# Part of the output stored early, two buffers for the P rows, phases on ScalarE and a new written order, in a kernel that mixes two long convolutions

## The chip, the cores and the metric

The kernel runs on one core of one Trainium2 chip. The core has five engines that run side by side: TensorE (PE, with its weight loads shown as PEld), VectorE (DVE), ScalarE (ACT), GpSimd (POOL) and SyncE (SP, which here only issues DMAs), and 16 DMA engines that they share. The metric is the device time of one execution in microseconds (us). The kernel before took 279.8 us, the median of three runs (279.80, 280.59 and 277.46).

## The reference

For an input x of 2048 rows and 448 channels, the reference computes two long causal convolutions along the rows and mixes them with a gate:

```
g = sigmoid((x * gate_w).sum(-1))                       # one gate per row
K[d, l] = Re sum_n C[d,n] * exp(dt[d]*A[d,n]*l) * dt[d]*B[d,n]     # 256 modes, 2048 taps
a = irfft(rfft(x, 4096) * rfft(K, 4096))[:2048] + x * Dskip
kv = (sum over t of k shifted by t rows * shift_k[:, 3 - t ...]) * v   # 4 taps
b = x * (irfft(rfft(kv, 4096) * rfft(ssm_k, 4096))[:2048] + kv * ssm_D)
out = g * a + (1 - g) * b
```

A is complex, so K needs an exponential and a sine and cosine for every channel, mode and level. Below, "A" names the convolution whose taps K the kernel must generate, and "B" the one whose taps ssm_k come as an input.

## The kernel before

The 448 channels lie as 4 groups of 112 on 4 x 32 partitions. The 112 columns of a group are worked in 4 chunks of 28 (`NQG`, `NC`), so there are eight convolutions, B and A of each chunk. A convolution is done by TensorE as a factored Fourier transform: `spread` (first stage, PSUM tile `ps_c`), `transform` (second stage, `ps_2`), a product with the transformed taps on VectorE (`products`, which also needs a copy of the tile with its real and imaginary halves exchanged by DMA, `swapped`), then the inverse, `stage_a` (`ps_a`) and `stage_b` (`ps_b`). ScalarE carries nearly every PSUM tile to SBUF. The tiles between the stages, 128 x 32 x 112 in bf16 (names `zs`, `zsS`, `zsK`, `U`), share one pool of `NBQ` = 7 buffers. The temporary tiles of the front part use it too.

The taps K of A come in 8 blocks of 14 columns (`KGen.block`). A chunk of two blocks has its tables of exponentials and phases (`Tables.levels`, `Tables.reals`): for each power level a phase is made on VectorE as an integer turn (`unit`, tile `ks_ph`, or `ks_ph4` for the first chunk), its low 16 bits go through a Sin on ScalarE, and VectorE multiplies with the Exp. From them VectorE builds two factor tables, the Q rows (`kg_TQ`, once in a chunk) and the P rows (`kg_TP`, once in a block, 32 rows of 2 x 112), and TensorE multiplies the two (`pk`). P rows 8 to 15 are a sum of two products: VectorE writes both, and a DMA issued by GpSimd adds one onto the other. Rows 16 to 31 (`back`) are made from rows 0 to 15. There is one P tile, so a block's rows cannot be written while the matmuls of the block before it still read them. `gather` (`ps_g`) rounds the taps into place, and `spread` with `WcK` starts their transform.

The inverse's matrix G (`Consts.stage_b`) is made in the front from eight phase instructions (`sb_ph`), four Sin and sixteen masks. The gate's two factors are `gb` and `og`; `mix` scales and adds the A and B results of the first three chunks in place, in tile `vt` (also called `ug`). The last convolution, A of chunk 3, runs in halves; its epilogue adds to the last 28 columns, 16 rows of each partition at a time, and `store` then writes those rows with all 112 columns, on SyncE and ScalarE in turns.

The sequence of all of this is written out by hand. Every engine call is first collected in a list by `Order`, and `ORDER` names the list's indices in the sequence in which they are issued; each engine then runs its own instructions in just that sequence, waiting where data are not there. All instructions therefore have line 148, and the profile is read by the names of tiles.

Of the kernel before, what the change touches and what calls it, by code (L numbers as in the profile page):

```python
# [9 lines left out]
ACT = mybir.ActivationFunctionType  # L10
# [28 lines left out]
NBQ = 7  # L39
# [3 lines left out]
    "0-1 540 2 945 947 23 886 559 533 553-554 896-897 560 31 13 544 538 542-543 967 36 946 539 546 549 60 12 551 22 "  # L43
    "561 563 565 569 955 562 8 970 566 61 953-954 25 62-68 572-580 831 934 931 928 529 3 930 938 7 564 53 34-35 557 "
    "601-605 568 606-609 32 582-589 33 30 531 962 541 545 548 581 4 9 17 29 936 958 591 914 905 44 889 907 550 887 "
    "941 590 874 851 878 527-528 11 555 850 864 968 956 926 833 556 619-623 929 830 592-599 860 863 924 855 28 927 "
    "829 600 843 859 836 835 834 610-614 14 24 839 948 898-899 949 877 530 942 842 837 950 832 933 838 27 615-617 "
    "932 923 957 879 16 624-627 618 854 847 873 960 861 963 875 628 865 868 26 20 70 41 848 631 535 844-845 18 880 "
    "567 532 840 849 906 964 69 630 470-497 19 937 629 299-326 925 888 883 558 959 876 852-853 916 185-212 915 866 "
    "856-857 965 858 890 869-870 547 891 882 862 867 908 1500 498-525 42 900 570 871 917 885 918 872 327-354 841 971 "  # L50
    "213-240 43 961 966 881 355 55 552 241 10 15 5 21 6 951 526 356-411 58 939 534 536 38 242-297 884 128-155 57 56 "
    "943 412 909 846 39 952 537 298 2873 2887 2883 40 571 2884 46 413-440 1478 2885 441-469 2896 37 54 632 935 "
    "156-184 2888 71-98 2895 2877 99-127 910 892 921 913 2878 911 2876 940 912 1480 47 684-692 893 920 903 650-666 "
    "633-648 667-679 919 680-682 649 683 765-771 895 772-781 1479 2882 48 45 748-764 711-719 731-737 720-727 738-746 "
    "728 782-789 894 969 747 1151-1164 790 1483 1165-1166 901 904 1125-1140 1486 922 1481 1167 902 49 51 1142-1150 "
    "1141 791-799 693-701 1491 1202-1209 702-710 944 1108-1124 1482 2874 1502 1210 1168-1181 1501 1182-1183 "
    "1091-1103 1484 1503 1104-1106 52 50 1184-1191 1107 809-816 1489 1192-1200 817 800-807 1201 59 972-1001 1504 "
    "1271-1278 808 1002-1016 1279 1490 1505 2875 1298-1305 1487 1017-1031 1306 1506 1032-1046 1493 1307-1315 1507 "
    "1047-1061 818-826 1494 1508 1062-1084 2880 1316-1323 1495 729 1085-1086 1324 1492 2563-2569 1325-1333 2570-2578 "
    "1496 2579 1485 1883-1890 1499 1891 1849-1862 1488 1498 1476 1497 2879 1510 1863-1864 2881 1334-1342 730 2889 "  # L60
    "1509 1511 1280-1287 1289-1296 1512-1543 1865 1297 2897 1544-1639 1473 828 1640-1703 2900 1704-1735 1288 2899 "
    "2901 827 2118-2119 2904 1736 2905-2906 2120 1245-1261 2909 2121 2908 2910 2919 2122 2918 2123 1228-1244 "
    "1262-1269 2892 1270 2920 2124 2886 1211-1218 1474 2893 2126 1475 2125 2890 1219-1227 2911 2128 1477 2922 "
    "2537-2544 1755-1794 2545 2902 2520-2535 1795 1408-1439 2907 2536 2486-2502 2898 2894 2503-2519 2903 1440-1455 "
    "1828 1456-1471 2923 1737-1753 2924 1343-1358 2912 2921 1359-1390 2914 2913 1391-1406 1472 2127 1754 1866-1872 "
    "2915 2891 1829 2946 2928 2927 2129 2937 1814-1821 2969 2943 1873-1879 2938 2934-2935 2933 2666-2673 2929 2674 "
    "2916-2917 2940 1407 2930 1880-1882 2925 2130-2161 1831 2162-2193 1830 2194-2225 1832-1845 2675-2682 1846-1848 "
    "2683 2947 2944 2226-2353 2948 2971 1909-1916 1822 2949 2932 1823-1826 2354 2926 2970 1827 1952-1960 2945 2941 "
    "1805-1812 1943-1951 2693-2701 1917-1925 2931 2952 1892-1907 1926-1941 2942 2972 1813 1942 2936 2955 1908 "
    "2546-2552 2973 2553-2561 4620-4626 2958 2974 1796-1803 2959 4627-4628 2684-2691 2597-2604 2975 2939 2562 2605 "  # L70
    "1804 2692 2580-2595 2962 2950 2373-2413 1961-1968 1970-1977 2596 1969 1978 2711-2718 2355-2371 2702-2709 2719 "
    "4145 4153 2720-2727 2963 2951 2961 2053-2068 2710 2069-2116 2964 2976 2965 2372 2977 2728 2979 4149 2729-2737 "
    "2432-2439 4152 2440 2968 2953 1988-2019 2966 4148 4151 4147 2960 2954 2020-2035 4186 4150 3298 2117 2423-2431 "
    "2956 2967 2036-2051 2978 3318-3324 2980 4146 2957 4176 3352-3359 4154 3360 2981-3044 4177 3587 4185 4187 3297 "
    "3045-3076 3300 3299 2441-2444 3077-3108 4167 2445 4178 2870 3325-3334 4168 1979-1987 4169 2414-2422 3109-3172 "
    "4160 4159 4161 3173-3205 2466-2473 2052 4180 3589 3588 2474 3361-3368 4165 4164 4166 3412-3420 3590 3395-3402 "
# [968 lines left out]
```

## Time and profile before

| | |
|---|---|
| median of three runs | 279.8 us |
| the profiled execution, and its span | 277.69 us, 275.8 us |
| busy: DVE, ACT, PE, PEld, POOL | 241.7, 226.7, 210.7, 193.3, 15.9 us |
| packets of all DMAs | 55110, 24.74 MB; 49680 of them under 512 bytes |
| stores of the output | 16 DMAs of 112 KB, 8 by SyncE and 8 by ScalarE |
| P rows' adding DMA (`kg_TP<-kg_P`) | 8 DMAs of 448 KB, 5.7 us from issue to landing |
| loads of ScalarE's function tables | 11, 1283 ns each |

The page of a profile gives busy time by engine, then a line of 40 digits for each engine, in which a digit is the busy share of a fortieth of the span in tenths. Groups of instructions are listed as out<-in with the number of instructions, their busy time and the mean duration of one. A list of waits says which instruction stood, what it waited for, the total in us, how many times and the longest. A timeline line is start, duration, engine, operation.

### The profile page before, as it was taken

What the parts mean: (1) busy time and instruction counts of PE and PEld (TensorE: products, weight loads), DVE (VectorE), ACT (ScalarE), POOL (GpSimd) and SP (SyncE); (2) the same over time, 40 slices, a digit from 0 to 9 for tenths busy, and PEclk for the clock granted to TensorE, in tenths of its full rate; (3) what the DMA queues carried; (4) which work ended last, traced back from release to release, by engine and by line L of the source; (5) the groups of instructions that cost most, each with busy time, mean ns of one, the idle gap of its engine ahead of it and who ended that gap; (6) DMA issues with size and microseconds to landing.
All of it is one profiled execution on the core that took longest, in us unless ns stands there. A gap on an engine that the chain in (4) does not pass through costs nothing.

```text
span 275.8 us, 12739 instructions
## 1 busy us (share of the span) xinstructions
PE 210.7 (76%) x5770; PEld 193.3 (70%) x5770; DVE 241.7 (88%) x488; ACT 226.7 (82%) x383; POOL 15.9 (6%) x51
## 2 busy tenths in 40 slices
PE   0610958879988799798997789867887999699830
PEld 0500858877887798687995779766886899688820
DVE  7599899999989799979996899899999997967950
ACT  2795696999899999998998799999999989546400
POOL 8000000000400000100010001001001001000000
PEclk9999999999999899998998999999999999979975
DMA  7999799607804500390093019003042263600077
GB/s 149 224 204 172 131 235 175 99 1 153 118 5 91 116 5 4 83 186 5 5 209 47 5 50 199 10 2 70 6 90 64 54 138 60 147 5 2 2 141 127
DMA packets 55110, 24.74 MB, mean 90 GB/s; under 512 B 49680, under 2 KB 52368, under 8 KB 55056
## 3 DMA queue, kind: packets, MB, share of 16 engines
q1 hardware_dynamic: 48640, 19.34, 37.7%
q0 software_dynamic: 1152, 3.67, 7.2%
q10 hardware_dynamic: 5264, 0.92, 2.1%
q8 instruction: 45, 0.74, 1.2%
q14 instruction: 9, 0.07, 0.1%
HBM read 7.95 MB, written 2.87 MB: 39 GB/s over the span
## 4 chain that ended last, share of the span: by engine, by line
ACT 38%; PE 29%; DVE 15%; DMA 9%; issue 5%; SPq 0%; DVEq 0%; POOL 0%; POOLq 0%; ACTq 0%
ACT zs L148 15%; ACT ET L148 7%; ACT U L148 6%; DMA kg_TP<-kg_P 6%; PE pk L148 5%; PE ps_a L148 5%; PE ps L148 5%; PE ps_c L148 5%; PE ps_b L148 5%; ACT zsK L148 5%; DVE vt L148 2%; DVE scratch L148 2%; PE ps_g L148 2%; PE ps_gate L148 2%; DMA skraw<-in_B_ssm_k_dram 2%
## 5 line engine op out<-in xcount | busy, mean ns | idle before, releaser
L148 ACT CAST zs<-ps 128x896 bf16<-128x896 f32 x48 | 44.0, 944 | 1.0 <-PE ps L148 0.6
L148 ACT CAST zs<-ps_c 128x1024 bf16<-128x1024 f32 (+1 forms) x48 | 42.7, 937 | 1.3 <-PE ps_c L148 1.2
L148 PEld LDWEIGHTS <-front 128*32 128x32 bf16 (+1 forms) x496 | 19.1, 159 | 27.3 <-issue 22.3
L148 PEld LDWEIGHTS <-s_W 128*128 128x128 bf16 x544 | 28.9, 100 | 12.7 <-issue 9.6
L148 PE MATMUL pk<-kg_TP,kg_TQ 128*32 128x32 bf16 x1792 | 33.2, 242 | 5.1 <-issue 2.9
L148 PEld LDWEIGHTS <-kg_TQ 128*32 128x32 bf16 x1792 | 31.2, 160 | 7.0 <-issue 4.8
L148 PE MATMUL ps_a<-sa_R,zs 128*128 128x128 bf16 x224 | 32.7, 235 | 0.3
L148 ACT CAST U<-ps_a 128x1024 bf16<-128x1024 f32 (+1 forms) x30 | 27.2, 936 | 6.9 <-PE ps_a L148 6.7
L148 PE MATMUL ps_b<-U,sb_G 128*128 128x28 bf16 x1024 | 29.5, 175 | 4.1 <-issue 1.4
L148 PE MATMUL ps_a<-sa_R,zsS 128*128 128x128 bf16 x224 | 32.1, 232 | 0.5 <-DVE zsS L148 0.5
L148 PE MATMUL ps<-zs,s_W 128*128 128x112 bf16 x384 | 27.7, 220 | 5.5 <-ACT zs L148 4.2
L148 PEld LDWEIGHTS <-sb_G 128*128 128x128 bf16 x1024 | 27.8, 96 | 5.8 <-issue 3.2
L148 DVE TENSOR_TENSOR kg_TP<-kg_TP,ET 128x1792 bf16<-128x1792 bf16 x24 | 26.1, 1090 | 5.8 <-DMA kg_TP<-kg_P 5.0
L148 PEld LDWEIGHTS <-zsS 128*128 128x128 bf16 x224 | 29.6, 152 | 1.3 <-DVE zsS L148 0.7
L148 PEld LDWEIGHTS <-zs 128*128 128x128 bf16 x224 | 29.4, 151 | 0.8
L148 PE MATMUL ps_v<-front 128*32 128x336 bf16 (+3 forms) x448 | 16.0, 310 | 16.0 <-DVE front L148 13.1
L148 ACT ACTIVATE ET<-ks_ph 128x448 bf16<-128x448 int16 x40 | 23.2, 602 | 4.1 <-DVE kg_P L148 2.6
L148 DVE TENSOR_TENSOR kg_TQ<-kg_TQ,ET 128x896 bf16<-128x896 bf16 (+1 forms) x36 | 24.8, 730 | 0.0
L148 DVE TENSOR_TENSOR kg_P<-kg_TP,ET 128x1792 bf16<-128x1792 bf16 (+1 forms) x24 | 22.4, 934 | 0.1
L148 PE MATMUL ps_c<-Wc,uu 128*64 128x128 bf16 x224 | 18.4, 290 | 1.6 <-ACT U L148 0.6
L148 PE MATMUL ps_c<-Wc,vt 128*64 128x128 bf16 x224 | 17.1, 285 | 1.4 <-ACT zs L148 1.2
L148 PEld LDWEIGHTS <-uu 128*64 128x64 bf16 x224 | 16.5, 210 | 2.4 <-issue 1.5
(102 smaller groups left out, 427.4 us busy)
## 6 DMA issues: line engine op xcount, KB each, us to landing
zsS<-zs SPq DMA_DIRECT2D x16, 448.0 KB, 5.7
kg_TP<-kg_P POOLq DMA_DIRECT2D x8, 448.0 KB, 5.7
vt<-in_B_v_dram SPq DMA_DIRECT2D x4, 448.0 KB, 6.8
skraw<-in_B_ssm_k_dram SPq DMA_DIRECT2D x16, 112.0 KB, 4.8
uu<-in_A_u_dram SPq DMA_DIRECT2D x4, 448.0 KB, 8.5
ks_xf<-xfd SPq DMA_DIRECT2D x3, 336.0 KB, 3.3
out_dram<-vt ACTq DMA_DIRECT2D x8, 112.0 KB, 3.8
out_dram<-vt SPq DMA_DIRECT2D x8, 112.0 KB, 3.6
```

Source lines behind the costliest of these rows:

```text
L148: ins = f(*args, **kw)
```

## The change

1. `store` writes only the last 28 columns of the rows that are just done. The 84 columns of the first three chunks are written by four new DMAs on SyncE at the end of `mix`.
2. One P tile of 48 rows takes the place of one of 32: rows 0 to 15 exist twice, by the block's parity, rows 16 to 31 (`late`) once. The pool of big tiles goes from 7 buffers to 6.
3. In the last block, rows 8 to 15 are made as the lower rows are, with two products and two sums on VectorE, and no DMA.
4. The phases of the first chunk's tables (20 instructions) and of G (8) are computed by ScalarE as a scaled and shifted copy, with the shifts in four constants that GpSimd sets; 12 negations in the tables and the four additions of ssm_D to the loaded ssm_k go to VectorE, from ScalarE and GpSimd.
5. `ORDER` is a new sequence of the 6767 calls (6758 before). The reading of it here is by index: calls up to the last block's P rows moved by 4, later ones by 5, those after `mix` by 9.

```diff
-NBQ = 7
+NBQ = 6
...
+        self.turns = {x: self.carve(1).bitcast(f32) for x in (0.0, QUARTER, 8192.0, 8192.0 + QUARTER)}
+        for x, t in self.turns.items():
+            nc.gpsimd.memset(t, x)
...
-                self.phases(ph[:, :, r, :], jv, k_col, o)
+                nc.scalar.activation(ph[:, :, r, :], jv, ACT.Identity, scale=k_col[:, 0:1], bias=o)
...
+    def summed(self, dst, src, r, m):
+        n = src.shape[1]
+        part = self.pool.tile([P, 8 * 2 * M], bf16, name="kg_P4", tag="kg_P4", bufs=2)[:, 0:n * 2 * m]
+        for c, out in enumerate((part.rearrange("p (n v m) -> p n v m", n=n, v=2), dst)):
+            self.nc.vector.tensor_tensor(out=out, in0=src[:, :, c].unsqueeze(2).to_broadcast([P, n, 2, m]),
+                                         in1=bass.AP(r.tensor, r.offset + c * m, [list(r.ap[0]), [0, n], [-m, 2], [1, m]]), op=ALU.mult)
+        self.nc.gpsimd.dma_start(dst.rearrange("p n v m -> p (n v m)"), part, accum_op=ALU.add)
...
-        TP = self.pool.tile([P, 32, 2, M], bf16, name="kg_TP")
+        if j == 0:
+            self.TA = self.pool.tile([P, 48, 2, M], bf16, name="kg_TP")
+        TP, late = self.TA[:, 16 * (j % 2):16 * (j % 2) + 16], self.TA[:, 32:48]
+        far = 16 * (2 - j % 2)
...
-            V.tensor_tensor(out=TP[:, 16 + i0:16 + i1], in0=src,
+            V.tensor_tensor(out=late[:, i0:i1], in0=src,
...
+        if j == NBLK - 1:
+            add(8, mult(TP[:, 0:4], 64))
+            add(12, mult(TP[:, 4:8], 64))
+        else:
+            self.summed(TP[:, 8:16], TP[:, 0:8], EP[:, entry_of(64) - EQ_N + 1], M)
...
-                V.tensor_scalar(out=o, in0=f, scalar1=e * turn, scalar2=off + (QUARTER if c == first else 0.0),
-                                op0=ALU.mult, op1=ALU.add)
+                shift = off + (QUARTER if c == first else 0.0)
+                if h:
+                    V.tensor_scalar(out=o, in0=f, scalar1=e * turn, scalar2=shift, op0=ALU.mult, op1=ALU.add)
+                else:
+                    nc.scalar.activation(o, f, ACT.Identity, scale=e * turn, bias=self.cons.turns[shift])
...
-                    nc.scalar.mul(B[:, :, 2], B[:, :, 0], -1.0)
+                    V.tensor_scalar(out=B[:, :, 2], in0=B[:, :, 0], scalar1=-1.0, scalar2=None, op0=ALU.mult)
...
-        nc.gpsimd.tensor_tensor(out=raw[:, :, 0], in0=raw[:, :, 0], in1=dB[:, H * NC:(H + 1) * NC], op=ALU.add)
+        V.tensor_tensor(out=raw[:, :, 0], in0=raw[:, :, 0], in1=dB[:, H * NC:(H + 1) * NC], op=ALU.add)
...
-    def store(b0, n):
+    def store(b0, n, c0, c1):
         for g in range(4):
-            dmae[g % 2].dma_start(out4[g][:, b0:b0 + n, :], ug[g * 32:(g + 1) * 32, b0:b0 + n, :])
+            dmae[g % 2].dma_start(out4[g][:, b0:b0 + n, c0:c1], ug[g * 32:(g + 1) * 32, b0:b0 + n, c0:c1])
...
-            store(b0, n)
+            store(b0, n, (NQG - 1) * NC, 112)
...
+        done = (NQG - 1) * NC
+        for g in range(4):
+            nc.sync.dma_start(out4[g][:, :, 0:done], ug[g * 32:(g + 1) * 32, :, 0:done])
```

In the new order VectorE's `mix` of the third chunk has 22 VectorE instructions behind it, where it had 8, and the inverse of A's third chunk is issued ahead of that of B's fourth. On VectorE the C-times-B products of the front have 47 instructions ahead of them, where they had 73, and on ScalarE the first copy of a spread has 86 ahead, where it had 63.

## The prediction

> **What bounds the kernel now.** I read the page's forty slices first, then the busy time of each engine in four stretches, then VectorE's waits, then the end.
>
> ```profile
> DVE  7599899999989799979996899899999997967950
> ACT  2795696999899999998998799999999989546400
> ...
> DMA  7999799607804500390093019003042263600077
> ```
>
> VectorE (DVE) and ScalarE (ACT) are at 8 or 9 tenths from slice 7 to slice 33; the DMA engines are full at the front and once more in the last two slices, where every other engine stands still. The stretches, with columns PE, PEld, DVE, ACT, POOL, granted clock, DMA share and GB/s:
>
> ```profile
> 0.00:45.00 45.00, 19.57 (x451) 17.75 (x455) 39.16 (x136) 30.35 (x58) 6.67 (x41) 1.00 1.07 185
> 45.00:240.00 195.00, 168.90 (x4659) 154.63 (x4654) 181.32 (x323) 185.60 (x312) 9.19 (x10) 0.97 0.38 74
> 240.00:262.00 22.00, 20.16 (x608) 18.94 (x601) 17.47 (x24) 10.73 (x14) 0.00 (x0) 0.92 0.02 4
> 262.00:276.00 14.00, 2.09 (x84) 1.99 (x80) 3.78 (x8) 0.00 (x0) 0.00 (x0) 0.61 0.75 132
> ```
>
> Up to 45 us ScalarE has 14.7 us idle while VectorE has 5.8. From 45 to 240 both are at 93 to 95%, so work taken from one alone moves the end little unless its waits go too. After 262 VectorE does 3.8 us of the 14. What VectorE waited for:
>
> ```profile
> DVE kg_TP L148 <- DMA kg_TP<-kg_P: 5.0, 3, 2.1
> ...
> DVE kg_KT L148 <- PE ps_g L148: 3.4, 1, 3.4
> ...
> DVE kg_TP L148 <- PE pk L148: 1.4, 2, 0.8
> ```
>
> The 5.0 us are the accumulating DMA that fills P rows 8 to 15 (5.7 us from issue to landing), the 1.4 us the matmuls that still read the only P tile. At the end:
>
> ```profile
> 262.85 8.95 SPq L148 DMA_DIRECT2D out_dram<-vt  x8
> ...
> 265.84 0.39 DVE L148 TENSOR_TENSOR vt<-ept,vt 128x448 bf16<-128x448 bf16 x1
> ```
>
> VectorE's last instruction ends at 266.23, SyncE goes on issuing stores until 271.8, and the span ends at 275.8: 9.6 us of pure storing.
>
> **The change part by part.** The sum is made against the profiled execution: 277.7 us, a span of 275.8 with 1.9 around it. That is 2.1 us below the median, 279.8; I subtract the same gain from the median.
>
> *The stores.* Today 16 DMAs carry 112 columns, 8192 packets of 224 bytes. Queues 1 and 10 from 262 to 276 us, with packets, MB and share of 16 engines:
>
> ```profile
> q1 hardware_dynamic: 4224, 0.92, 39.4%
> q10 hardware_dynamic: 4224, 0.92, 35.4%
> ```
>
> 74.8% of 16 engines for 14 us is 167.6 us for 8448 packets: 19.8 ns each, so 512 on each engine take 10.1 us, which is the tail. Afterwards the same 8192 packets carry 56 bytes. No row has such a store. The nearest are loads: in 143 to 147 us queue 1 moves 123 bytes a packet, in the first 5 us queue 10 moves a few bytes a packet:
>
> ```profile
> q1 hardware_dynamic: 1863, 0.23, 42.1%
> ```
>
> ```profile
> q10 hardware_dynamic: 709, 0.00, 8.2%
> ```
>
> These are 26.9 us / 1863 = 14.5 ns and 6.6 us / 709 = 9.3 ns. Between them 56 bytes come to 11.6 ns, 5.9 us for 512. The last of them cannot leave before VectorE ends: 266.3, an issue of 0.7 us and 3.6 to land give 270.6 instead of 274.5. I take **-4.0 us**; the ends are -4.2 (landing only) and +2. The +2 comes from the four new DMAs of 84 columns, 8192 packets again, 10.1 us at 19.8 ns. In the new order the addition that frees them has 22 VectorE instructions behind it (14.4 us by their rows, 13.0 with the 0.064 us by which neighbours overlap) and the first small store leaves about 3 us before VectorE ends, so they have 10 us alone; if VectorE runs through without a wait, the last packets meet the small stores. On SyncE only those stores stand behind them.
>
> The Trainium skill (DMA: Bandwidth & Descriptors, Specifications) says that a transfer under 512 bytes is a read-modify-write, which speaks against a split into 168 and 56 bytes. The 224-byte packets are under that limit already, so the rows cannot show whether 56 bytes cost less; it is the first rival.
>
> *The phases.* 20 instructions on 224 elements and 8 on 512 leave VectorE for ScalarE; their rows, under that of a ScalarE Exp of equal width:
>
> ```profile
> L148 ACT ACTIVATE ET<-early 128x224 bf16<-128x224 f32 x16 | 5.5, 386 | 2.4 <-DVE early L148 2.4
> ...
> L148 DVE TENSOR_SCALAR sb_ph<-scratch,sb_offs 128x512 int32<-128x512 int32 x8 | 5.1, 633 | 0.2
> ...
> L148 DVE TENSOR_SCALAR ks_ph<-early 128x224 int32<-128x224 f32 x20 | 4.5, 267 | 3.0 <-ACT early L148 3.0
> ```
>
> VectorE loses 4.5 + 5.1 us in all and gains 12 negations (8 x 0.274 + 4 x 0.215 = 3.1, by its own 448- and 224-element rows), four small additions from GpSimd (0.6) and, in the last block, two products and two sums instead of two products and a DMA (2 x 0.625 = 1.25): 241.7 becomes 237.1. ScalarE has no such row; the nearest of equal width are the Exp above (386 ns) and a 512-element copy (617): 20 x 0.386 + 8 x 0.617 = 12.7 us. Against it stand 3 early negations (1.7) and two table loads of 1.283: the list of groups counts 11, and the new order changes between Sin and Exp 9 times. A scaled copy in between (the negations) has no load of its own today. Net +8.4 us on ScalarE, in a stretch with 14.7 idle: hidden. If that cover is gone, it is the second rival.
>
> The Trainium skill (ScalarE: Activation LUTs, Rules for kernel authors) gives plain products and sums to VectorE and budgets about 0.3 us plus 0.83 ns an element on ScalarE; by that estimate the 28 cost 15.6 us instead of 12.7, still under the idle time.
>
> *What VectorE gains in front.* Before, from the first C-times-B product at 17.58 to the end of the last v product at 48.50, it runs 68 instructions without a gap. The new order has 47 small ones ahead (9.4 us) and again 68 up to that v product, 33.5 us by rows, 29.2 with overlap. Its start hangs on the second ks_b, 28th on ScalarE with 11.5 us of work behind the first PSUM result at 8.5: 17.4 to 20. I keep 17.6, so v ends at 46.8: **-1.7** (to +0.7). Behind it now stand 363 instructions with 206.9 us instead of 347 with 203.2: **+3.7**.
>
> *Waits that come to VectorE and SyncE.* The four additions to the ssm_k loads wait for DMAs; GpSimd stood 45.8 us for them with nothing urgent behind it, on VectorE all the rest would stand. The latest, before the fourth convolution, has its load behind the last ks_xf load on SyncE, issued at 163.1 before, so landed by 169; it now stands next to a P-row product that ran at 175.0. Some 6 us of cover, cost nothing; without it up to the 4.8 us of landing. On SyncE one v load passes the four k transposes, 0.6 us of issue; the first convolution matmuls waited for VectorE's diagonals until 27.7, which hides it.
>
> *P rows in two buffers.* The next block's rows can be computed, and their DMA land, while the matmuls read the last block's: the 5.0 and the 1.4 us go, **-6.4** (ends 0 and -9.8, with the 3.4 us for ps_g, where mixing work is now placed). What is late next is TensorE. After the last block's pk matmuls it has 461 matmuls, 17.8 us, up to 264; in the new order 645, about 24.8. For a body 4.4 us shorter they must end at 234.7, 11.5 earlier. VectorE's last P row has 9.7 us less work ahead of it and 14 instructions fewer, 8.8 net, and 6.4 of waits: it can.
>
> *Six big tiles instead of seven.* The timeline shows seven such tiles between first write and last read for most of 147 to 217 us. VectorE's other waits behind 48.5 are 14.5 - 6.4 = 8.1 us; if they grow as the look-ahead shrinks, by a sixth, **+1.3** (0 to +15). GpSimd's four constants (0.1 us each, beside the first loads) cost nothing; without that cover 0.4.
>
> Sum: -4.0 - 1.7 + 3.7 - 6.4 + 1.3 = -7.1. The profiled execution gives 270.6, the median **272.7**.
>
> **Rivals.** *Packets priced by count*: the 56-byte store takes 19.8 ns as the 224-byte one does, the tail stays 9.6 us: 272.7 + 4.0 = 276.7. For it: the loads' rows are not stores. Against: 9.3, 14.5 and 19.8 ns rise with size.
>
> *ScalarE becomes the front's bound*: the 28 phases sit before the Sin that feeds the first spread, and its idle time was waiting, not room. The whole 8.4 us come through: 281.1, no change. For it: 86 ScalarE instructions before the first zs copy instead of 63. Against: they need 42 us by rows, less with overlap, and that copy ran at 48.0.
>
> *Six tiles stall the convolutions*: slower. The spread of the next convolution can't be evacuated until the pair before it has been swapped (5.7 us), multiplied (2.02) and read. One such wait on the path is 7.7 us, two 15.4: 288.1. It decides from the second, since 9.9 us make 1% slower. For it: seven in use today. Against: ScalarE and VectorE have 14 and 9 us of waits in 195, none of which names a buffer.
>
> *A scaled-and-shifted copy has a table of its own*: 36 loads instead of 9, 27 x 1.283 = 34.6 us: 307. The negations speak against it.
>
> **How the numbers follow.** Forecast 0.56, the rivals in this order 0.12, 0.12, 0.18, 0.02. Runs of before spread by 1.1%, so about 1% (277.0 to 282.6) is what can be told from no change. Faster: 0.56 and half of the first rival, 0.62; within 1%: its other half and the second, 0.18; slower: 0.20. The best ends (-4.2, all 14.5 us of waits gone, +2.0) give 263; with 2 in 10 left out the range is 265 to 285, the top just past one stall. The forecast's own range is 267 to 277.
>
> **What would show it.** Right: no VectorE wait on the P rows' DMA, VectorE near 237 us, 9 table loads, v done by 47, about 5.6 us from VectorE's last instruction to the end. Wrong: small-store packets at 20 ns, ScalarE full before 45 with v after 48, or new waits of 5 us and more on the swaps between 100 and 235.

## The result, and the profile after

The changed kernel takes **297.3 us** (median; 296.8 to 299.6), the kernel before 278.6 in the same session: a ratio of 1.069 (95% interval 1.058 to 1.079). It is slower, where 272.7 was forecast, and it lies outside the range.

The profiled execution of after took 296.8 us with a span of 295.0. VectorE's last instruction ends at 276.84 instead of 266.23 (+10.6), and from there to the end of the span it is 18.2 us instead of 9.6 (+8.6). These two numbers make the 19.2 us between the spans. The forty slices of after, for VectorE, ScalarE and the DMA engines:

```profile
DVE  7167599999699798999989999879399899769400
ACT  2956999988998889999998999998993795654000
DMA  7999899041943605520363205030360050449994
```

VectorE now has a hole in slices 2 to 5 (7 to 37 us: 1, 6, 7 and 5 tenths), where the kernel before has 5, 9, 9 and 8, and the DMA engines end with 9, 9, 9 and 4 tenths instead of 7 and 7. The stretches of after, cut where VectorE ends, with columns as before:

```profile
0.00:45.00 45.00, 16.98 (x313) 14.83 (x317) 29.22 (x102) 32.84 (x69) 6.26 (x43) 0.92 1.06 183
45.00:240.00 195.00, 169.36 (x4535) 155.06 (x4528) 176.88 (x338) 179.71 (x302) 6.44 (x7) 0.92 0.36 67
240.00:262.00 22.00, 18.48 (x622) 16.92 (x621) 17.61 (x18) 15.24 (x22) 0.00 (x0) 1.00 0.23 53
262.00:277.00 15.00, 11.25 (x311) 10.69 (x310) 13.42 (x22) 4.64 (x6) 0.00 (x0) 0.86 1.18 98
277.00:295.00 18.00, 0.00 (x0) 0.00 (x0) 0.00 (x0) 0.00 (x0) 0.00 (x0) 0.50 0.93 24
```

Up to 45 us VectorE is busy for 29.2 us instead of 39.2: it gave 9.6 us of phases away and stands idle for 15.8 us instead of 5.8. In the last line no engine computes, the DMA engines are busy for 93% of 18 us, and they move 24 GB/s; the 14 us at the end of before moved 132. What VectorE waited for in after, longest first:

```profile
DVE ks_tC_re L150 <- PE ps_m L150: 8.5, 1, 8.5
DVE kg_P L150 <- DMA kg_TP<-kg_P: 7.5, 3, 4.4
DVE kg_TP L150 <- DMA kg_TP<-kg_P: 5.0, 3, 2.2
DVE ET L150 <- ACT ET L150: 4.2, 3, 3.4
DVE kg_TP L150 <- PE pk L150: 3.1, 3, 1.6
```

The 5.0 us for the accumulating DMA are still there to the tenth, and 7.5 us of a new kind stand beside them: VectorE wants to write a `kg_P` tile that the DMA has not yet read out. The wait for `pk`, for which the second buffer was made, is 3.1 us instead of 1.4. Which instructions stood there, in before and then three in after (start, duration, engine, operation; in brackets the idle time just ahead and what ended it):

```profile
147.35 1.09 DVE L148 TENSOR_TENSOR kg_TP<-kg_TP,ET 128x1792 bf16<-128x1792 bf16 x1 [2.14 <-DMA kg_TP<-kg_P]
```

```profile
196.54 1.09 DVE L150 TENSOR_TENSOR kg_TP<-kg_TP,ET 128x1792 bf16<-128x1792 bf16 x1 [2.16 <-DMA kg_TP<-kg_P]
...
213.19 1.09 DVE L150 TENSOR_TENSOR kg_P<-kg_TQ,ET 128x1792 bf16<-128x1792 bf16 x1 [4.44 <-DMA kg_TP<-kg_P]
...
236.56 0.63 DVE L150 TENSOR_TENSOR kg_TP<-kg_P 128x896 bf16<-128x896 bf16 x1 [1.65 <-PE pk L150]
```

All three waits of the 5.0 us are of the first kind, in before as in after: the product that makes rows 16 to 23 (`back(0, 8)`) reads rows 15 to 8 of its own block, to which the DMA is still adding. A second copy for the next block cannot shorten that wait; only other work put between the two can. The 4.44 us are the longest of the new kind, and the product that waits there is one of the Q rows. The 1.65 us end with the last matmuls of the seventh block, while VectorE writes rows of the eighth, which lie in the other copy. Why they wait at all is not shown; the matmul's operand in that block reaches from the first copy across the second to the upper rows, so a dependency kept by that reach would give it.

The stores, from the timeline (start, duration, engine) and from the DMA queues between 262 and 296 us (packets, MB, share of 16 engines):

```profile
261.54 27.85 SPq L150 DMA_DIRECT2D out_dram<-vt  x12
...
276.44 0.39 DVE L150 TENSOR_TENSOR vt<-ept,vt 128x448 bf16<-128x448 bf16 x1
```

```profile
q1 hardware_dynamic: 12480, 1.61, 75.5%
q10 hardware_dynamic: 4224, 0.23, 24.6%
```

From its first store to its last SyncE takes 27.85 us, waits for VectorE among them. Together the queues hold all 16 engines for the whole 34 us: 544 us of engine time for 16704 packets, 32.6 ns each, where the 224-byte packets of before took 19.8.

VectorE's end can be split in each kernel into its work (time in which it runs an instruction) and its idle time. Read so from the traces, in us, for all runs in which the body matters:

```
                            work   idle to 55   idle after 55    ends    tail    span
before                     241.7       5.8          18.7        266.2     9.6   275.8
after                      237.1      16.5          23.2        276.8    18.2   295.0
before_scalar_phases       233.8      20.6          17.2        271.6     9.8   281.4
before_inverse_phases      237.4       7.3          17.3        261.9     9.8   271.7
before_last_block_direct   243.0       6.7          15.8        265.5     9.7   275.2
before_three_edits         238.4       8.0          16.7        263.2     7.7   270.8
after_whole_stores         237.2      17.5          26.4        281.1    10.8   291.9
after_whole_vector_phases  244.5      11.4          21.9        277.8    10.6   288.4
after_whole_direct_rows    245.4      17.6          10.4        273.4    10.1   283.5
after_whole_seven_tiles    237.0      18.8          22.0        277.7    10.5   288.2
seven_tiles_front_before   244.6       9.2          23.6        277.4    10.1   287.5
seven_tiles_front_direct   253.1       9.9          12.3        275.4    10.1   285.5
after_split_at_80          236.9      18.9          22.7        278.5     6.9   285.4
after_split_at_80_direct   245.4      18.1          11.5        275.0     6.7   281.7
```

For after against before: 4.6 us less work, 10.7 more idle time in front and 4.5 behind it, sum +10.6.

### The profile page after: what moved, and what is told of

Its sections match the earlier page's. It is cut to its first block, busy times and chain, and to the rows that moved or that the text cites. A ratio compares the mean times of both kernels' runs of the same rounds, so it can differ in the third digit from the quotient of the medians.

```text
span 295.0 us, 12741 instructions
## 1 busy us (share of the span) xinstructions
PE 216.1 (73%) x5770; PEld 197.5 (67%) x5770; DVE 237.1 (80%) x478; ACT 232.4 (79%) x397; POOL 12.7 (4%) x50
## 5 line engine op out<-in xcount | busy, mean ns | idle before, releaser
L150 PE MATMUL pk<-kg_TP,kg_TQ 128*32 128x32 bf16 x1792 | 35.4, 242 | 11.4 <-DVE kg_TP L150 6.2
L150 PEld LDWEIGHTS <-kg_TQ 128*32 128x32 bf16 x1792 | 32.2, 160 | 14.0 <-issue 6.0
L150 PEld LDWEIGHTS <-front 128*32 128x32 bf16 (+1 forms) x496 | 20.2, 160 | 30.5 <-issue 23.3
L150 PEld LDWEIGHTS <-s_W 128*128 128x128 bf16 x544 | 29.3, 100 | 11.4 <-issue 8.2
L150 PE MATMUL ps_a<-sa_R,zs 128*128 128x128 bf16 x224 | 34.0, 241 | 1.1 <-DVE zs L150 0.7
L150 PE MATMUL ps_a<-sa_R,zsS 128*128 128x128 bf16 x224 | 33.0, 238 | 0.8 <-DVE zsS L150 0.8
L150 PE MATMUL ps_v<-front 128*32 128x336 bf16 (+3 forms) x448 | 17.9, 328 | 16.2 <-ACT ks_ph L150 9.0
L150 DVE TENSOR_TENSOR kg_TP<-kg_TP,ET 128x1792 bf16<-128x1792 bf16 x23 | 24.8, 1084 | 5.0 <-DMA kg_TP<-kg_P 5.0
L150 DVE TENSOR_TENSOR kg_P<-kg_TP,ET 128x1792 bf16<-128x1792 bf16 (+1 forms) x25 | 23.3, 934 | 2.7 <-DMA kg_TP<-kg_P 2.6
L150 ACT CAST zsK<-ps_c 128x512 bf16<-128x512 f32 (+3 forms) x27 | 17.2, 637 | 9.9 <-PE ps_c L150 9.9
L150 DVE TENSOR_TENSOR kg_TQ<-kg_TQ,ET 128x896 bf16<-128x896 bf16 (+1 forms) x36 | 24.7, 717 | 0.0
L150 DVE TENSOR_TENSOR kg_P<-kg_TQ,ET 128x1792 bf16<-128x1792 bf16 (+1 forms) x20 | 17.7, 895 | 4.5 <-DMA kg_TP<-kg_P 4.4
```

Source lines behind the costliest of these rows:

```text
L150: ins = f(*args, **kw)
```

## The experiments on the stores

**The split undone, and the small stores by themselves.** Both start from the changed kernel. In `after_whole_stores` the early store goes and the late ones are whole:

```
-        done = (NQG - 1) * NC
-        for g in range(4):
-            nc.sync.dma_start(out4[g][:, :, 0:done], ug[g * 32:(g + 1) * 32, :, 0:done])
...
-            store(b0, n, (NQG - 1) * NC, 112)
+            store(b0, n, 0, 112)
```

> The changed kernel with one part undone: no early store of 84 columns, the last convolution stores all 112 columns in 224-byte packets as before. Theory A (the split itself makes the long end: the 84-column packets and the 28-column packets share the DMA engines after 261 us): the stretch from VectorE's last instruction to the end of the span falls from 18.2 to about 9.6 us and the time from 297.3 to 288.7, ratio to the kernel before 1.036. Rival B (the stores are slow because the body ends late or the DMA engines are slower in this run, not because of the split): the end stays near 18 us and the time near 297. VectorE's last instruction should in both cases end near 276.8.

Measured 291.7 us, ratio 1.047 (1.039 to 1.055), tail 10.8 us. Theory A holds for the tail; the gain is 5.6 us between the medians, not 8.6, since VectorE ended at 281.1 in this profile. VectorE's end moves by some us between executions (the four spans of this run lie between 287.9 and 291.9), so tails are read from the traces and totals from the medians.

`after_small_stores_alone` leaves out only the three lines of the early store.

> The changed kernel with the early store left out, so 84 of each group's 112 output columns are never written; the 56-byte packets have the DMA engines for themselves. Priced by size (11.6 ns a packet, my prediction): 5.9 us for 512 packets on each engine, an end of about 5.6 us, 284.7. Priced by count (19.8 ns as the 224-byte packets): an end of 9.6 us, 288.7. Dearer than 224-byte packets (32 ns, the mean in the crowded profile): 16.4 us, an end near 17, 296.

Measured 290.7 us (two runs, ratio 1.046), tail 12.4 us in the profile (289.3). The whole rows of `after_whole_stores` had a tail of 10.8 with four times the bytes, so neither of the first two prices holds. The 56-byte packets are dearer than those of 224 bytes (24.7 ns against 19.6), as the third price says, but the time lies nearer the second (288.7) than the third (296). Their times explain it: the median is 11 ns, just the price that was forecast (11.6), but the mean is more than twice that, because 462 of 8192 take 100 ns or more, some over 1000, and hold 113 of 202 us. Before 276 us 3755 packets had gone with 4 such among them, after it 4437 with 458.

**The split in the kernel before.**

```
+        done = (NQG - 1) * NC
+        for g in range(4):
+            nc.sync.dma_start(out4[g][:, :, 0:done], ug[g * 32:(g + 1) * 32, :, 0:done])
...
-            store(b0, n)
+            store(b0, n, (NQG - 1) * NC, 112)
```

> The kernel before with the split of the stores alone, everything else and the order unchanged: four 84-column DMAs on SyncE after the addition that ends at 261.66, then 28-column stores from 262.8. Theory A (the split costs): the end grows from 9.6 to about 18 us, 279 + 8.6 = 287.3, ratio 1.031. Rival B (the split is harmless and the body's order is what made the end long): 279, ratio 1.00. My prediction's price (11.6 ns, the 84-column packets gone in 10 us before the small ones): 275.

Measured 292.9 us, ratio 1.055 (1.048 to 1.062): this edit alone costs the kernel before 14.6 us. VectorE ends at 266.5 as ever, the tail is 24.6 us. Theory A, and more than it said, since here the early store has no start on the late ones.

**The two sets kept apart.** The first two chunks, 56 columns, are ready at 245.95, so they are stored there, 17 us ahead of the late 56:

```
+            if H == 1:
+                for g in range(4):
+                    nc.sync.dma_start(out4[g][:, :, 0:2 * NC], ug[g * 32:(g + 1) * 32, :, 0:2 * NC])
...
-            store(b0, n)
+            store(b0, n, 2 * NC, 112)
```

> The kernel before with another split: the first 56 columns of each group are stored in 112-byte packets after the addition that ends at 245.95, 17 us before the first late store, so the two sets cannot meet; the last 56 columns are stored late, also in 112-byte packets. Priced by size (about 13.5 ns a packet): an end of 6.5 us, 279 - 3 = 276. Priced by count (19.8 ns): 279, no change. Dearer when smaller (26 to 32 ns): an end of 13 to 16 us, 282 to 285.

Measured 285.1 us, ratio 1.021 (1.011 to 1.030): the third price. The sets did not meet, so collision is not the cause, and still 799 of 16384 packets took 100 ns or more.

**Number or kind of packets.** 16384 packets again, all of 224 bytes; the extra ones go to a scratch tensor:

```
+        for g in range(4):
+            nc.sync.dma_start(spare[g], ug[g * 32:(g + 1) * 32, :, :])
```

> The kernel before with 8192 more store packets, but of 224 bytes: after the addition that ends at 261.66 four DMAs on SyncE copy all 112 columns as they then are to a scratch tensor of the output's shape, and the stores of the result follow whole. In before_split_stores 16384 packets of 168 and 56 bytes took 24.9 us from the first to the last, 658 a us, and packets of 100 ns and more made up much of it. Theory S (packets under 224 bytes are what the memory takes slowly, once some 4000 have gone): 16384 packets of 224 bytes go at the 800 to 1000 a us of the kernel before, 16 to 20 us, almost none over 100 ns, an end of 13 to 17 us after VectorE, 282 to 286. Rival N (the number of packets is what counts): 25 us and an end of 24 us as in before_split_stores, 293.

Measured 292.3 us, ratio 1.050, which by itself would speak for rival N. The trace says otherwise: VectorE ended at 280.9 because its last additions wait until the copy has read their columns, as the first of its waits says, and the tail behind it is 9.1 us.

```profile
DVE vt L145 <- DMA spare<-vt: 13.0, 1, 13.0
```

Of 16384 packets none took 100 ns, the mean is 19.6. The total of this run cannot be compared; its packets can, and they hold for theory S.

**Size or ends.** Pieces of 56, 112 and 168 bytes are no multiples of 32 bytes, 224 is one. So one size of `before_half_early` is changed, 56 | 56 columns to 48 | 64:

```
-                    nc.sync.dma_start(out4[g][:, :, 0:2 * NC], ug[g * 32:(g + 1) * 32, :, 0:2 * NC])
+                    nc.sync.dma_start(out4[g][:, :, 0:48], ug[g * 32:(g + 1) * 32, :, 0:48])
...
-            store(b0, n, 2 * NC, 112)
+            store(b0, n, 48, 112)
```

> before_half_early with one size changed: the early part is 48 columns (packets of 96 bytes), the late part 64 columns (packets of 128 bytes), so that all pieces start and end at multiples of 32 bytes, as those of 224 bytes do and those of 56, 112 and 168 do not. Theory M (pieces that are no multiple of 32 bytes are what stalls): no packets over 100 ns, 8192 late ones at about 12 ns on 16 engines = 6.1 us instead of 10, an end of 6 to 7 us after VectorE, 275. Rival Z (every packet under 224 bytes stalls once some 4000 have gone): an end near 13 us and 283 to 285, as in before_half_early.

Measured 276.4 us, ratio 0.9945 (0.9916 to 0.9974), tail 7.5 us. The queues from 263 to 280 us, with 56 late columns (`before_half_early`):

```profile
q1 hardware_dynamic: 4224, 0.46, 53.1%
q10 hardware_dynamic: 4224, 0.46, 33.5%
```

and with 64 (`before_half_48`):

```profile
q1 hardware_dynamic: 4224, 0.52, 24.8%
q10 hardware_dynamic: 4224, 0.52, 20.8%
```

As many packets and more bytes take 45.6% of 16 engines instead of 86.6%. Theory M holds. The same one size in the changed kernel, 84 | 28 columns to 80 | 32:

```
-        done = (NQG - 1) * NC
+        done = 80
...
-            store(b0, n, (NQG - 1) * NC, 112)
+            store(b0, n, 80, 112)
```

> The changed kernel with one size changed: its early store takes 80 columns instead of 84 (160 bytes), its late ones 32 instead of 28 (64 bytes, multiples of 32). Theory M (pieces that are no multiple of 32 bytes stall): no packets over 100 ns, the early 8192 gone within 10 us, the late ones at about 10 ns, an end of 6 to 8 us after VectorE instead of 18.2: 297.3 - 11 = 286. Rival (two sets of 8192 packets are too many whatever their ends): 292 to 297.

Measured 287.6 us, ratio 1.034 (1.027 to 1.040), tail 6.9 us. The queues from 262 to 296 us, as shown for after above:

```profile
q1 hardware_dynamic: 12480, 1.57, 31.7%
q10 hardware_dynamic: 4224, 0.26, 9.4%
```

41.1% of 16 engines instead of 100.1 for the same number of packets. Four columns moved from one store to the other are worth 9.7 us, and the split as such is then a gain, some 4 us against whole rows. The packets of these runs, by size, from the traces:

```
bytes   packets   median   mean    of 100 ns or more         kernel
  224      8192     16 ns   20.1      0                        before
  224     16384     16      19.6      0                        before_whole_twice
  160      8192     13      15.3      0                        after_split_at_80
  128      8192     13      14.8      1                        before_half_48
   96      8192      9      11.7      0                        before_half_48
   64      8192     11      11.6      1                        after_split_at_80
  168      8192     15      31.1    416, with  92.5 us         after
  112     16384     13      25.8    799, with 186.9 us         before_half_early
   56      8192     11      34.0    584, with 182.4 us         after
   56      8192     11      24.7    462, with 113.0 us         after_small_stores_alone
  168      8192     15      32.3    459, with  96.8 us         before_split_stores
   56      8192     11      22.7    314, with  86.0 us         before_split_stores
```

The aligned pieces of all other runs show at most three of 8192 packets at 100 ns or more. Two things these runs do not separate. In SBUF the pieces are cut at the same columns of rows of 224 bytes, so the border could be one of the source as well as of the target. And each stalling piece is both of a length that is no multiple of 32 bytes and off that border at one end at least.

The Trainium skill (Collectives: The Full Stack, Rules for kernel authors) asks for buffers aligned to 32 bytes, with the reason "Prevents HW read-modify-write"; it says so of collectives, and these rows show the same border for plain stores. The Trainium skill's other rule, weighed in the prediction (DMA: Bandwidth & Descriptors, Specifications: below 512 bytes a read-modify-write), does not part the rows: all of them are under 512.

## The experiments on the phases and the front

**All 28 phases on ScalarE, nothing else.**

```
-                self.phases(ph[:, :, r, :], jv, k_col, o)
+                nc.scalar.activation(ph[:, :, r, :], jv, ACT.Identity, scale=k_col[:, 0:1], bias=o)
...
-                V.tensor_scalar(out=o, in0=f, scalar1=e * turn, scalar2=off + (QUARTER if c == first else 0.0),
-                                op0=ALU.mult, op1=ALU.add)
+                if h:
+                    V.tensor_scalar(out=o, in0=f, scalar1=e * turn, scalar2=shift, op0=ALU.mult, op1=ALU.add)
+                else:
+                    nc.scalar.activation(o, f, ACT.Identity, scale=e * turn, bias=self.cons.turns[shift])
```

> The kernel before with the 28 phase instructions of the first chunk and of the inverse on ScalarE, nothing else changed; its order stays, with four constants set by GpSimd at the start. Theory A (the phases delay ScalarE in front, 28 x 0.40 to 0.80 us = about 15 us, more than the 14.7 us that it has idle before 45): later v products and zs copies, 278 + 5 = 283. Rival B (they are innocent: VectorE, 93% busy behind the front, loses 9.6 us of work): 270 to 275. My prediction's working would give -4 to -5 us: about 274.

Measured 284.5 us, ratio 1.0225 (1.017 to 1.028): theory A. The first 45 us and VectorE's longest waits of `before_scalar_phases`:

```profile
0.00:45.00 45.00, 14.73 (x270) 12.87 (x274) 26.39 (x95) 38.35 (x79) 6.45 (x44) 0.99 0.92 170
```

```profile
DVE ks_tC_im L145 <- ACT ks_b L145: 7.8, 1, 7.8
DVE ET L145 <- ACT ET L145: 4.3, 4, 2.1
DVE early L145 <- ACT ks_ph L145: 4.1, 1, 4.1
```

ScalarE is busy for 8.0 us more, VectorE for 12.8 less: the second copy `ks_b`, which VectorE's C-times-B products need, ran at 15.18 before and now runs at 17.51, behind nine phases. The v products end at 55.7 instead of 48.5. VectorE's 7.9 us of saved work bought 14.8 us of idle time in front.

**Only the 8 phases of the inverse, and those in gaps.** The first edit of the two above, with the eight, and the four Sin that use them, placed in the order where ScalarE stood idle before:

> The kernel before with only the 8 phase instructions of the inverse on ScalarE, each in a gap of ScalarE's that the trace of before shows (4.6 to 8.6, 18.3 to 19.6, 24.6 to 25.9, 26.3 to 28.7, 29.1 to 30.4, 31.6 to 32.5 and 42.4 to 45.0 us), the four Sin of the inverse put in the order in which their phases are now ready; the 20 phases of the first chunk stay on VectorE. Theory G (ScalarE can take work where the order leaves it in a gap; what cost 6 us in before_scalar_phases were the chunk's 20 in front of their Sin): VectorE has 4 to 5 us less to do, the last v product ends near 45, the time falls by 3 to 4 us to 274.5. Rival (ScalarE is the front's bound whatever it is given): 8 x 0.80 = 6.4 us more on it, 278 to 284.

Measured 274.7 us, ratio 0.986 (0.980 to 0.991): theory G, a gain of 3.4 us. The first 45 us and the v products of `before_inverse_phases` (durations min, median, max; first and last start):

```profile
0.00:45.00 45.00, 22.36 (x520) 19.95 (x521) 37.69 (x133) 38.60 (x71) 6.88 (x40) 1.00 1.06 181
```

```profile
L145 DVE TENSOR_TENSOR vt<-ps_v,vt x8: 1082/1086/1093, 34.1 to 44.5; 128x896 bf16<-128x896 f32 x8
```

ScalarE is as full as in the run before, 38.6 us against 38.35, and TensorE is 7.6 us of work further on at the same instant. The last v product ends at 45.6. So some of ScalarE's idle time was room, enough for the 6.4 us of these eight. The two runs differ in the number of phases as well as in their places, so that the places alone decide is argued from the waits on `ks_b` and `ks_ph` above, not shown.

**The phases given back in the changed kernel.** `after_whole_stores` with the two edits above reversed, at the same places of the order.

> The changed kernel with whole stores (as in after_whole_stores, ratio 1.047, 291.7) and, besides, the 28 phase instructions back on VectorE, at the same places of the order. Theory A (ScalarE took the phases in a stretch in which VectorE then waited for it: by the busy time done up to 45 us VectorE stood 5.6 us further back than in the kernel before): the last v product ends near 48.5 instead of 52.0 and the time falls by about 5 us, to 286. Rival B (the phases are innocent, the new order of the front is slow by itself): VectorE has 9.6 us more to do, the last v product ends at 52 or later and the time is between 292 and 301.

Measured 290.9 us, ratio 1.046 (1.041 to 1.052): no gain over 291.7. In the table, idle time in front falls from 16.5 us (after) to 11.4, but work grows by 7.4, and the last v product ends at 54.4. Neither theory's time came, though the v product is where rival B has it. The new order keeps VectorE waiting for the C-times-B matmuls (6.4 us here, 8.5 in after) whoever does the phases.

**The front in the old order.** The old front has seven big tiles in use, so this is made with seven (see below): some 930 of the first 1000 calls in the order of before, phases on VectorE and the four additions on GpSimd.

> after_whole_seven_tiles (ratio 1.044, 290.4; its upper P rows read other factors, so the output isn't the reference's) with the first 60 us in the kernel before's order on every engine, the 28 phases on VectorE and the four ssm_D additions on GpSimd; behind that the changed kernel's order. Theory O (what the body lost is the new order of the front: VectorE waits 8.5 us for the C-times-B matmuls where it ran phases before): last v product back from 53 to 48.5 and 5 to 6 us less, 285. Rival (the later order would lose the time anyway, because TensorE or ScalarE set its pace): 290.

Measured 288.7 us, ratio 1.035 (1.029 to 1.041), against 290.4 with seven tiles alone: a gain of 1.7, not 5 to 6, and the intervals of the two ratios still overlap. The last v product ends at 50.8 instead of 54.2, not at 48.5. The idle time in front does fall by 9.6 us (18.8 to 9.2), and VectorE's work rises by 7.6 with the phases that come back. The phases' 9.6 us and the front's idle time are one trade here, and with the changed kernel's order behind the front VectorE gains nothing from it.

## The experiments on the P rows

**No accumulating DMA.** `after_whole_stores` with rows 8 to 15 of every block made as in the last one:

```
-        if j == NBLK - 1:
+        if j >= 0:
             add(8, mult(TP[:, 0:4], 64))
             add(12, mult(TP[:, 4:8], 64))
```

> The changed kernel with whole stores and with rows 8 to 15 in all eight blocks as in its last one: two products and two sums on VectorE, no accumulating DMA at all. VectorE gets 7 x 1.25 = 8.75 us more work. Theory W (its 12.5 us of waits for that DMA, 5.0 of the rows and 7.5 of the part buffer that the DMA holds, stand on the path): 291.7 + 8.75 - 12.5 = 288. Rival (the waits only stood where VectorE would have waited for TensorE anyway): 291.7 + 8.75 = 300, with TensorE's wait for the rows as long as before.

Measured 287.1 us, ratio 1.034 (1.027 to 1.040), 4.6 us under `after_whole_stores`: theory W, within a microsecond. The longest waits of VectorE in this kernel:

```profile
DVE ks_tC_re L147 <- PE ps_m L147: 8.5, 1, 8.5
DVE ET L147 <- ACT ET L147: 4.0, 3, 3.4
DVE kg_TP L147 <- PE pk L147: 2.7, 3, 1.6
```

Both rows with the DMA are gone and none has taken their place: behind the first 55 us VectorE is idle for 10.4 us, where `after_whole_stores` has 26.4, after 23.2 and before 18.7. So two buffers and direct rows do give VectorE a body with fewer gaps, for 8.3 us of work more.

**Seven big tiles.** Room is made by letting the 16 growth factors share two places:

```
-NBQ = 6
+NBQ = 7
...
-EP_N = 2 + 3 * len(P_LEVELS) + NR
+EP_N = 2 + 3 * len(P_LEVELS) + 2
...
-                            in1=EP[:, E_R - EQ_N + i0:E_R - EQ_N + i1].unsqueeze(2).to_broadcast([P, i1 - i0, 2, M]), op=ALU.mult)
+                            in1=EP[:, i0 % 8:i0 % 8 + 8].unsqueeze(2).to_broadcast([P, i1 - i0, 2, M]), op=ALU.mult)
...
-            self.exps(self.EP[:, :, E_R - EQ_N + i], 8 * (2 * i + 1))
+            self.exps(self.EP[:, :, E_R - EQ_N + i % 2], 8 * (2 * i + 1))
```

> The changed kernel with whole stores and seven big tiles instead of six. Room for the seventh is made by leaving work's results out: the 16 growth factors of the upper P rows are computed by the same instructions but share two places, and the products of these rows read eight other factors, so that the output isn't the reference's; number, size and order of the instructions stay. Theory T (the seventh tile was what let the swaps start early: with six, the last two swaps start at 235.59 and 253.86, within 0.1 us of the last read of another big tile, with seven they started at 220.3 and 232.3): these two start 10 us and more sooner, and the time falls by one or two stalls of 7.7 us, to 276 to 284. Rival (the order sets the pace, six tiles are enough): 291.7, with the swaps at most a few us sooner.

Measured 290.4 us, ratio 1.044 (1.039 to 1.049), against 291.7: the rival. The last two swaps start at 237.0 and 251.5, where they start at 239.2 and 258.3 in `after_whole_stores`, and the time hardly moves. VectorE's waits for the DMA stay:

```profile
DVE kg_P L147 <- DMA kg_TP<-kg_P: 7.3, 3, 4.4
DVE kg_TP L147 <- DMA kg_TP<-kg_P: 3.9, 3, 2.2
```

**Old front and direct rows together.**

> seven_tiles_front_before and, besides, rows 8 to 15 by two products and two sums in all blocks, without the accumulating DMA (that alone was 4.6 us off in after_whole_direct_rows). If both causes add up: 285 - 4.6 = 280, level with the kernel before. If the waits for the DMA were long only because VectorE came late in front: 285.

Measured 285.7 us, ratio 1.025 (1.019 to 1.031). The direct rows are worth 3.0 us here, and the sum stays 6 us above the 280 expected. By the table VectorE is idle for 22.2 us in all, less than in before, but it has 253.1 us to do instead of 241.7. So VectorE's end comes later by its work: 8.5 us of it direct rows (against `seven_tiles_front_before`), the rest mostly the 3.1 us of negations.

**One block direct in the kernel before.**

> The kernel before with one part of the change alone: rows 8 to 15 of the last block by two products and two sums on VectorE instead of two products and the accumulating DMA, and the last product of its P rows moved directly behind. In the kernel before that last product ran at 235.69 to 236.78, after the DMA issued at 231.14; now 228.51 + 3.43 + 2.2 = 234.1. If the last block's rows are on the path: 278.3 - 2.5 = 276. If TensorE (22.5 us busy of the last 24.4 before 264) sets the end: 278.3, no change. If the 1.25 us more of VectorE count: 279.5.

Measured 277.7 us, ratio 0.998 (0.995 to 1.0015): nothing that can be told from no change. VectorE ended 0.7 us sooner in the profile, with 1.3 us more work, which fits the second expectation, TensorE as what sets the end.

**What the experiments add up to.** The two mends of the changed kernel in one, stores split at 80 columns and direct rows:

> after_split_at_80 and, as in after_whole_direct_rows, no accumulating DMA. If both gains add: 286 - 4.6 = 281.5, within 1.5% of the kernel before. If the early stores were in the way of the accumulating DMA or of the swaps only in the old form: 286.

Measured 283.4 us, ratio 1.018 (1.012 to 1.024), 4.2 under `after_split_at_80`: the gains add, to 2 us less than hoped. From 297.3 us the four columns of the stores took 9.7 and the accumulating DMA 4.2; what is left is 5.4 us above the 278.0 of the kernel before in that session. The body is 8.8 us longer than in before, 3.7 of them work, and the tail 2.9 shorter. And the kernel before with the three edits that helped there or did no harm, the inverse's phases in ScalarE's gaps, 48 columns early and the last block direct:

> before_half_48, before_inverse_phases and before_last_block_direct in one kernel. If theories M and G hold and the gains add: 278.2 - 3.3 - 3.7 - 0.4 = 271. If the stores gain nothing: 274; if neither does: 278 to 284.

Measured **271.7 us**, ratio 0.976 (0.970 to 0.981). It beats both kernels. Its slices, VectorE and the DMA engines:

```profile
DVE  7599699999989799979996899898999899987870
...
DMA  7999999909605400490092019103005350605447
```

VectorE is as busy in front as before the change, and the early store lies in slices 37 and 38, while VectorE still computes.

## Why the prediction was wrong, point by point

- **The sum.** Cut at the end of the last v product and at VectorE's last instruction, forecast and measured difference of the profiled executions are: front -1.7 and +3.5; VectorE's work behind it +3.7 and +2.5; its waits there -6.4 + 1.3 = -5.1 and +4.6; the tail -4.0 and +8.6. Together -7.1 and +19.2. Three steps failed, the stores, the P rows and the front; the work was nearly right.
- **Stores: -4.0 was +8.6, outside the bounds -4.2 to +2.** The failed step is "56 bytes come to 11.6 ns", a price between two loads, taken for a store. The median of the small packets is 11 ns, but the mean is 34, and no load showed what makes it: the stalls of pieces off the 32-byte border. The 84-column stores, put at 19.8 ns, took 31.1 for the same reason. With the one size mended the step holds nearly as forecast: 64-byte packets at 11.6 ns, a tail of 6.9 us where 5.6 were put. The first rival, packets priced by count, was wrong as well: aligned packets do get cheaper with size.
- **P rows: -6.4 was +9.2, outside 0 to -9.8.** The waits for the DMA and for `pk` that were to go are 15.6 us instead of 6.4. The failed step is "the 5.0 and the 1.4 us go". The 5.0 us stayed, because they are waits of a block for its own rows 8 to 15, which a copy for the next block does not touch. The 7.5 us are new, because the step forgot the other end of the DMA: it holds its source, one of two `kg_P` tiles through which the products of the P and Q rows pass, so the next rows stop where they need that tile. The kernel before has the same two tiles and no such wait; that the new order makes the difference is argued, not shown. The 1.4 us became 3.1. Without the DMA both of its waits are gone and 4.6 us are won (`after_whole_direct_rows`). The condition for TensorE failed with it: the last block's `pk` ended at 248.6 us, where 234.7 was needed.
- **Front: v ended at 52.0, not 46.8; -1.7 was +3.5.** The start was right, 16.97 for 17.6, and so was the work of the 68 instructions from there, 33.4 us by their rows and 28.8 with overlap for 33.5 and 29.2. The failed step is that they would again run without a gap: 6.2 us of idle time lie between them, put at nothing. The longest wait is for a Sin on ScalarE:

```profile
35.74 0.69 DVE L150 TENSOR_TENSOR ET<-ET,ks_mag 128x448 bf16<-128x448 bf16 x2 [3.43 <-ACT ET L150]
```

  The 8.5 us of waiting ahead of the first product were in the forecast, since its start was. By 55 us VectorE had been idle for 10.7 us more; the phases that it gave away are 9.6. How much of this is the phases and how much the new order is not settled: in the kernel before the 28 phases cost 6.1 us, in the changed kernel giving them back won nothing.
- **ScalarE.** The 28 phases cost 8.6 + 6.2 = 14.8 us, not 12.7 (474 and 804 ns, where 386 and 617 were taken). The lines of after:

```profile
L150 ACT ACT_TABLE_LOAD x9 | 11.5, 1283 | 1.9 <-issue 1.8
...
L150 ACT ACTIVATE ks_ph<-early,scratch 128x224 int32<-128x224 f32 x20 | 8.6, 474 | 5.7 <-DVE early L150 5.7
...
L150 ACT ACTIVATE sb_ph<-scratch,sb_offs 128x512 int32<-128x512 int32 x8 | 6.2, 804 | 0.0
```

  The Trainium skill's estimate in the prediction (ScalarE: Activation LUTs, Rules for kernel authors) was nearer; worked out again it is 15.5 us, not 15.6.

  Nine table loads came as counted, so the table rival fell. The second rival, ScalarE as the front's bound, is what `before_scalar_phases` shows in the kernel before: 284.5 us against 278.4 there, 6.1 lost, where the rival lets 8.4 through. "Hidden" in 14.7 us of idle time held for the 6.4 us of `before_inverse_phases`; that all 28 phases could be hidden there is not shown.
- **VectorE's work: 237.1 us, as forecast to the tenth.** It did not help: VectorE's idle time grew by 15.2 us.
- **Six tiles: +1.3 expected, 1.3 measured** by undoing it, less than its runs can tell from nothing, so that the two agree is luck. The slower rival (288.1) had the side right and the mechanism wrong. "New waits of 5 us and more on the swaps" did not appear among VectorE's; ScalarE has one of 6.5 us at 230 for a spread of the taps (`zsK<-ps_c`), and with seven tiles it has one of 6.6.
- **The four additions, the new place of the loads, the constants:** no wait of VectorE on an `skraw` load appears among its waits of 0.7 us or more. No cost shows, as put.

Not settled: the granted TensorE clock is 0.90 in after and 0.96 in before, 0.84 against 0.94 from 75 to 105 us, and TensorE is busy for 216.1 us instead of 210.7 with as many matmuls. No run separates cause and effect, so part of the last 5 us may be clock.

## What to carry to other kernels

Cut stores so that every piece begins and ends on a multiple of 32 bytes, in the source and in the target, and read the mean of a packet's time beside its median. Before a second buffer is credited with a wait, name every tile that the transfer holds, the source too. And ask which rows the waiting instruction reads: a wait of a block for its own rows is not lifted by a buffer for the next. Before work is moved to an engine with idle time, look whether an instruction that another engine waits for stands behind it; eight instructions put into gaps of the trace were free here, 28 put ahead of such instructions were not.

## What was not expected of the hardware

Stores of 56, 112 and 168 bytes have medians of 11 to 15 ns a packet; then, from some 2000 to 4000 packets on, single ones take 100 to over 1000 ns, in all one in 14 to 26. With 64, 96, 128, 160 or 224 bytes, 57344 packets of the table above hold two of 100 ns or more. The border is 32, not 16 and not 64: 112 is a multiple of 16 and stalls, 96, 160 and 224 are none of 64 and do not.

The Trainium skill (ScalarE: Activation LUTs, What ACT_TABLE_LOAD costs) puts an instruction at 186 ns + 0.833 ns an element and about 93 ns more for each operand, scale or bias, that it takes from a tile. For the 20 phases of 224 elements, with the bias from a tile, that is an estimate of 466 ns, and the rows show 474. For the eight of 512 elements, with scale and bias from tiles, it is 799 ns, and the rows show 804; so the page agrees, and the 0.3 us of the estimate in the prediction hold for one such operand.
